# Token-ordered loads of B and C by chunk, and one TensorE stretch per pair of chunks, in a Mamba-2 scan that feeds a GELU MLP

## The chip, the cores and the metric

One core of one Trainium2 chip. The metric is device time in microseconds (us); the profile adds the span of one profiled execution, which is about 2 us shorter than the time of the same run. Ratios are the mean time of one kernel's fast runs over that of the other's fast runs of the same rounds, with a 95% interval, so they are not quite the ratio of the medians that I quote. "Fast" and "slow" are states of a run: here a run over 1.5% above the fastest of its kernel counts as slow. PE is TensorE, DVE VectorE, ACT ScalarE, POOL GpSimd, SP SyncE, whose queue issues nearly all transfers.

## The reference

A gated linear scan in 4 batches of 8 heads, 768 tokens, head size 32, state size 16, then an MLP over all 3072 tokens (256 to 2048 to 256):

```python
for c in range(nc):                         # chunks of the sequence
    cum = np.cumsum(log_a[:, :, sl], axis=-1)
    L = np.exp(cum[:, :, :, None] - cum[:, :, None, :]) * causal
    M = np.einsum('bhin,bhjn->bhij', Cc, Bc) * L                  # Gram, masked
    y_intra = np.einsum('bhij,bhjd->bhid', M, xc)
    y_inter = np.einsum('bhin,bhnd->bhid', Cc, state) * np.exp(cum)[:, :, :, None]
    y[:, :, sl] = y_intra + y_inter
    state = decay_full * state + (B scaled)^T x                   # cut
h = y_tokens @ w_in                         # (3072, 256) @ (256, 2048)
out = gelu_tanh(h) @ w_out                  # (3072, 2048) @ (2048, 256)
```

The kernel works in 24 chunks of 128 tokens. B and C are scaled per token, so the Gram needs only a triangular mask.

## The kernel before

B and C of a whole batch come in one load each, with six neighbouring tokens on one partition. A contiguous run in memory is then 6 x 16 floats, 384 bytes. The price is the order of tokens: the scaled B must be transposed (for the Gram), evicted in token order, and transposed back (for the state product).

```python
def load_bc(b, i, q):                       # one batch, i = 0 for B, 1 for C
    q.dma_start(out=d["bc"][:, i],
                in_=(B, C)[i][b].rearrange("h (p r) n -> p h (r n)", r=R6))
...
def f_N(b, c0, c1):                         # B back to tokens on partitions
    for c in range(c0, c1):
        nc.tensor.transpose(out=bn_ps[...], in_=d["bh"][:, c * Q:(c + 1) * Q], identity=ident)
...
def f_G(gc):                                # Gram of one chunk: four row tiles, 32x128
    for g in range(4):
        nc.tensor.matmul(out=gb[:, g, 0:256], lhsT=d["bh"][32*g:32*g+32, ...],
                         rhs=d["ce"][32*g:32*g+32, :, ...], tile_position=(32 * g, 0))
...
def f_Y(gc):
    for w in range(2):                      # state part: the whole array, 128x128
        nc.tensor.matmul(out=y_ps[:, w], lhsT=sp[:, w*128:(w+1)*128], rhs=d["ch"][...], ...)
    for w in range(2):                      # chunk part: column tiles, 128x32
        for k in range(4):
            nc.tensor.matmul(out=y_ps[32*k:32*k+32, w], lhsT=x16[...], rhs=m[...],
                             tile_position=(0, 32 * k), ...)
    f_D(gc)                                 # state product: column tiles, lhsT = bn
```

Around this lies the MLP: `f_s1` (input product into one of two `hp` buffers in PSUM), `f_gelu` on ACT, `f_s2` (output product into `o_ps`), over groups of one or two chunks. The order of all instructions is fixed at build time by a list scheduler with estimated durations; PE works from that list and waits where the real data is later.

## Time and profile before

| kernel before | |
|---|---|
| time, median of 3 runs | 126.87 us (125.79 to 127.2) |
| span of the profiled execution | 125.3 us |
| PE busy | 117.3 us, 94% |
| first MLP matmul | 15.78 us |

The page cuts the span into 40 slices (3.1 us each), in tenths busy: PE, the granted PE clock, and DMA. Below them are the packets by size.

```profile
PE   5986989899999999999999999999999999999990
...
PEclk9985599999999999999999999999999999999998
...
DMA  3999999819997999931011101010110011001221
...
DMA packets 40047, 13.94 MB, mean 111 GB/s; under 512 B 33824, under 2 KB 39008, under 8 KB 40032
```

PE is at 0.8 or more from the fifth slice on, and the clock is at half in only two slices. DMA is busy for 17 slices, with one hole in the ninth, and then nearly idle. The same in two stretches of the span, with the columns length, then busy time (and count) of PE, weight loads, DVE, ACT, POOL, then granted clock, DMA share and GB/s:

```profile
28.00:40.00 12.00, 11.82 (x146) 9.59 (x145) 8.10 (x12) 7.83 (x16) 2.51 (x6) 1.00 1.02 183
40.00:60.00 20.00, 19.47 (x247) 15.70 (x246) 14.61 (x22) 14.04 (x29) 4.33 (x11) 1.00 0.76 138
```

The two dates to remember, from the timeline (start, length, engine, line, operation): the last cast of the weights `w_out`, and the cast of `x` of chunk 7.

```profile
24.52 0.69 DVE L243 CAST w_out_sb<-wf 128x1024 bf16<-128x1024 f32 x1
```
```profile
32.11 0.40 POOL L241 CAST x_607<-x_t 128x256 bf16<-128x256 f32 x1 [0.52 <-DMA x_t<-in_x_dram]
```

### The profile page before, as it was taken

Reading aid. Unit: us, or ns where it says so; the run is one execution under the profiler, and the core shown is the slowest. Engines: PE = TensorE matmul, PEld = TensorE weight load, DVE = VectorE, ACT = ScalarE, POOL = GpSimd, SP = SyncE. Lnnn points to the kernel's source line nnn. Section 1 sums busy time; section 2 is a strip of 40 time slices with the busy share of each in tenths; the row PEclk is TensorE's granted clock in tenths of the full one; section 3 lists DMA queues with packets and bytes.
Section 4 is the critical chain, followed back from the end, with each engine's and each line's share of the span. In section 5 each row is a group of like instructions: output and inputs, shape, how many; then the busy total and the mean of one; then the engine's idle time right before and its main releaser. Section 6 shows DMA issues by size and latency. Waiting matters only on the chain.

```text
span 125.3 us, 3171 instructions
## 1 busy us (share of the span) xinstructions
PE 117.3 (94%) x1326; PEld 92.3 (74%) x1327; DVE 66.9 (53%) x109; ACT 78.3 (62%) x162; POOL 21.4 (17%) x47
## 2 busy tenths in 40 slices
PE   5986989899999999999999999999999999999990
PEld 2552268689778878768788878787887888988970
DVE  5577777988656799735689650356524500000101
ACT  4021577694668666777749678778678777875110
POOL 6526756102411331111112000000000000000000
PEclk9985599999999999999999999999999999999998
DMA  3999999819997999931011101010110011001221
GB/s 83 264 338 324 297 290 291 196 51 156 164 287 120 170 273 136 153 65 50 7 35 45 42 2 47 0 42 5 42 42 18 29 42 42 25 19 47 84 84 44
DMA packets 40047, 13.94 MB, mean 111 GB/s; under 512 B 33824, under 2 KB 39008, under 8 KB 40032
## 3 DMA queue, kind: packets, MB, share of 16 engines
q1 hardware_dynamic: 38944, 13.29, 45.7%
q10 hardware_dynamic: 1088, 0.44, 1.4%
q8 instruction: 10, 0.16, 0.6%
q14 instruction: 5, 0.04, 0.1%
HBM read 10.58 MB, written 3.15 MB: 110 GB/s over the span
## 4 chain that ended last, share of the span: by engine, by line
PE 85%; DVE 7%; ACT 3%; issue 2%; DVEq 0%
PE hp L439 32%; PE o_ps L457 29%; PE o_ps L694 6%; PE yb L388 4%; PE gb L362 4%; PE hp L457 3%; PE hp L316 2%; DVE m L371 2%; DVE bc_188 L300 2%; PE yb L382 2%; PE yb L348 2%; ACT gT L447 1%; PE gb L268 1%; ACT bn L355 1%; DVE sp_new L420 1%
## 5 line engine op out<-in xcount | busy, mean ns | idle before, releaser
L447 ACT ACTIVATE gT<-hp 128x512 bf16<-128x512 f32 x96 | 55.4, 596 | 18.2 <-PE hp L439 17.4
L439 PE MATMUL hp<-xm,w_in_sb 128*128 128x256 bf16 (+1 forms) x416 | 55.0, 265 | 0.3 <-ACT gT L447 0.2
L457 PE MATMUL o_ps<-w_out_sb,gT 128*128 128x256 bf16 x352 | 50.1, 273 | 0.0
L439 PEld LDWEIGHTS <-w_in_sb 128*128 128x128 bf16 x416 | 36.3, 98 | 6.9 <-issue 0.7
L457 PEld LDWEIGHTS <-gT 128*128 128x128 bf16 x384 | 37.0, 98 | 4.6 <-issue 0.2
L371 DVE TENSOR_TENSOR m<-gb,tri 128x1024 bf16<-128x1024 f32 (+1 forms) x25 | 29.3, 1177 | 12.2 <-PE gb L362 12.0
L466 DVE COPY o_sb<-o_ps 128x256 f32<-128x256 f32 x2 | 0.8, 424 | 22.9 <-PE o_ps L457 22.9
L406 ACT ACTIVATE xm<-yb 128x256 bf16<-128x256 f32 x24 | 9.2, 383 | 5.1 <-PE yb L399 2.1
L420 DVE SCALAR_TENSOR_TENSOR sp_new<-s_new,pend,bmask 128x256 bf16<-128x256 f32 x20 | 10.7, 536 | 0.8
L414 DVE SCALAR_TENSOR_TENSOR s_new<-s_new,pend,yb 128x64 f32<-128x64 f32 x16 | 4.4, 277 | 12.0 <-ACT xm L406 6.1
L694 PE MATMUL o_ps<-wz 128*128 128x512 bf16 x20 | 8.2, 547 | 1.5 <-DVE warm L153 1.3
L464 ACT ACTIVATE o_sb<-o_ps 128x256 f32<-128x256 f32 x20 | 7.6, 381 | 2.8 <-PE o_ps L457 2.5
L362 PE MATMUL gb<-ce,bh 32*128 32x256 bf16 x96 | 7.1, 287 | 0.0
L382 PE MATMUL yb<-ch,sp_new 128*128 128x128 bf16 x40 | 5.5, 219 | 0.3
L355 ACT ACTIVATE bn<-yb 128x384 bf16<-128x384 bf16 (+2 forms) x9 | 4.1, 454 | 2.7 <-PE yb L348 2.7
L241 POOL CAST w_in_sb<-wf 128x1024 bf16<-128x1024 f32 x4 | 4.5, 1132 | 5.6 <-DMA wf<-in_moe_w_in_dram 5.6
L362 PEld LDWEIGHTS <-bh 32*128 32x128 bf16 x96 | 2.4, 91 | 4.0 <-issue 1.7
L694 PEld LDWEIGHTS <-wz 128*128 128x128 bf16 x21 | 2.3, 129 | 3.7 <-issue 2.2
L382 PEld LDWEIGHTS <-sp_new 128*128 128x128 bf16 x40 | 3.8, 98 | 1.0 <-issue 0.6
L457 PE MATMUL hp<-w_out_sb,gT 128*128 128x256 bf16 x32 | 3.8, 272 | 0.0
L464 ACT ACTIVATE o_sb<-hp 128x256 f32<-128x256 f32 x2 | 0.8, 384 | 4.5 <-PE hp L457 4.5
L348 PE MATMUL yb<-ident,bh 128*128 128x128 bf16 x24 | 2.9, 222 | 0.7 <-ACT xm L406 0.3
(157 smaller groups left out, 77.3 us busy)
## 6 DMA issues: line engine op xcount, KB each, us to landing
x_t<-in_x_dram SPq DMA_DIRECT2D x24, 128.0 KB, 3.9
out_dram<-o_sb SPq DMA_DIRECT2D x24, 128.0 KB, 1.7
wf<-in_moe_w_in_dram SPq DMA_DIRECT2D x4, 512.0 KB, 7.9
wf<-in_moe_w_out_dram SPq DMA_DIRECT2D x4, 512.0 KB, 7.2
bc_t<-in_C_dram SPq DMA_DIRECT2D x4, 384.0 KB, 4.3
bc_t<-in_B_dram SPq DMA_DIRECT2D x3, 384.0 KB, 4.9
bc_t<-in_B_dram ACTq DMA_DIRECT2D x1, 384.0 KB, 5.6
a_t<-in_a_dram ACTq DMA_DIRECT2D x1, 48.0 KB, 2.1
```

The lines of the kernel that those rows point to most:

```text
L348: nc.tensor.transpose(out=bn_ps[:, (c - c0) * 128:(c - c0 + 1) * 128], in_=d["bh"][:, c * Q:(c + 1) * Q], identity=ident)
L355: nc.scalar.activation(d["bn"][:, c0:c1].rearrange("p c n -> p (c n)"), bn_ps[:, 0:(c1 - c0) * 128], AF.Copy)
L362: nc.tensor.matmul(out=gb[:, g, 0:256], lhsT=d["bh"][32 * g:32 * g + 32, c * Q:(c + 1) * Q], rhs=d["ce"][32 * g:32 * g + 32, :, c * Q:(c + ...
L371: nc.vector.tensor_tensor(out=state[("m", gc)][:, g0:g1], in0=gram[:, g0:g1], in1=tri_b[:, g0:g1], op=ALU.mult)
L382: nc.tensor.matmul(out=y_ps[:, w], lhsT=sp[:, w * 128:(w + 1) * 128], rhs=d["ch"][:, c * Q:(c + 1) * Q], start=(w == 0), stop=False, skip_ ...
L406: nc.scalar.activation(xm[:, :, gc * Q:(gc + 1) * Q], y_ps, AF.Copy)
L420: nc.vector.scalar_tensor_tensor(out=sp_new.rearrange("p (g d) -> p g d", g=4), in0=state[("s", gc)].rearrange("p (o d) -> p o d", o=1).to ...
L439: nc.tensor.matmul(out=hp[:, j * nt:(j + 1) * nt], lhsT=w_in_sb[:, kc, fi * 128:(fi + 1) * 128], rhs=xm[:, kc, c0 * Q:c0 * Q + nt], start= ...
L447: nc.scalar.activation(gts[g][:, i * per:(i + 1) * per, 0:nt], hps.pop((g, i)).rearrange("p (j t) -> p j t", j=per), AF.Gelu_apprx_tanh)
L457: nc.tensor.matmul(out=ops[gc], lhsT=gts[g][:, fi, tt * Q:(tt + 1) * Q], rhs=w_out_sb[:, fi, :], start=(fi == 0), stop=(fi == NF - 1), ski ...
L464: nc.scalar.activation(o_sb, ops.pop(gc), AF.Copy)
L694: nc.tensor.matmul(out=zb, lhsT=wz[:, 0:128], rhs=wz, start=True, stop=True)
```

## The change

The intent is less work on PE. With B and C in token order, the scaled B is itself the weight of the state product, so the transposes back and their evictions go. Both parts of Y are then column tiles of one shape. From the pair of chunks 4 and 5 on, Y of one pair, the state product and the Gram of the next are issued in one go, so PE changes its tile shape three times a pair instead of six. The first chunk's work also needs only its own 128 tokens instead of a batch of 768.

```diff
-        q.dma_start(out=d["bc"][:, i],
-                    in_=(B, C)[i][b].rearrange("h (p r) n -> p h (r n)", r=R6))
+        for k in range(n):                       # n chunks of the unit, 128 tokens each
+            q.dma_start(out=BCF[u][:, i, k],
+                        in_=(B, C)[i][b, :, (c + k) * Q:(c + k + 1) * Q, :]
+                        .rearrange("h p n -> p h n"))
...
-    def f_N(b, c0, c1):  ...                     # and f_bn, its eviction on ACT
...
     def f_D(u):                                  # state product
-                             lhsT=U[b]["bn"][:, c, 32 * g:32 * g + 32],
+                                 lhsT=BC16[u][:, 0, k, 2 * g:2 * g + 2].rearrange("p h n -> p (h n)"),
...
     def f_Y(u):                                  # state part, now in column tiles too
-                nc.tensor.matmul(out=y_ps[:, w], lhsT=sp[:, w * 128:(w + 1) * 128], ...)
+                        nc.tensor.matmul(out=y4[32 * j:32 * j + 32, k, w],
+                                         lhsT=sp[:, 32 * h:32 * h + 32],
+                                         rhs=CE[u][:, h % 2, k], ...,
+                                         tile_position=(0, 32 * j))
...
+    MERGE = 3
+            def f_YDG(u):
+                f_Y(u)
+                f_D(u + 1)
+                f_G(u + 1)
...
+    load_x_n(0);  load_w_n(0, 1);  load_bc_n(1);  load_w_n(2, 3);  load_x_n(1)   # order on SP
+    load_bc_n(2); load_x_n(2);  load_w_n(0, 1, o=True);  load_bc_n(3)
+    load_w_n(2, 3, o=True);  load_x_n(3)
```

A run in memory is now 16 floats, 64 bytes.

## The prediction

> **What bounds the kernel now.** I read the busy shares first, then the chain of work that ended last, then stretches of the span, then one chunk of the scan in order of time, then the DMA.
>
> ```profile
> PE 117.3 (94%) x1326; PEld 92.3 (74%) x1327; DVE 66.9 (53%) x109; ACT 78.3 (62%) x162; POOL 21.4 (17%) x47
> ```
> ```profile
> PE 85%; DVE 7%; ACT 3%; issue 2%; DVEq 0%
> ```
> PE is the bound, in busy share and in the chain. But 94% is an average over stages, so I cut the span where chunk 7's Gram ends:
>
> ```profile
> 0.00:28.16 28.16, 24.37 (x261) 15.02 (x263) 20.88 (x41) 14.12 (x33) 12.97 (x28) 0.88 0.91 237
> 28.16:39.88 11.72, 11.54 (x144) 9.34 (x141) 7.82 (x12) 7.55 (x16) 2.51 (x6) 1.00 1.02 183
> 39.88:122.09 82.21, 81.42 (x928) 67.97 (x924) 37.81 (x57) 56.61 (x115) 5.88 (x13) 1.00 0.27 60
> ```
> Columns: length, then busy time of PE, weight loads, DVE, ACT, POOL, then granted clock, DMA share, GB/s. Up to 28 us the DMA is full (0.91) and PE is kept up with filler; after 40 us PE is full and DMA idle. So there are two problems. Late, only less PE work helps. Early, only bytes that arrive sooner help.
>
> The two MLP products, from 39.88 us to the end (first the one into the GELU, then the one out of it):
> ```profile
> 39.88:122.10 82.22, 43.05 (x300) 27.74 (x300) 1.00 0.27 60
> ```
> ```profile
> 39.88:122.10 82.22, 43.95 (x320) 31.03 (x320) 1.00 0.27 60
> ```
> Four of these matmuls take 0.4375 us start to start in the timeline, so 0.109 us each: 620 x 0.109 = 67.8 us. The scan's start-to-start time in the same stretch, summed from the timeline, is 12.6 us (Gram 3.62, state part of Y 3.05, rest of Y 2.10, state product 1.75, transposes 1.41 and 0.66). Together 80.4 of 82.2 us: 1.8 us are waits. The whole MLP costs 352 + 384 full matmuls and 64 half ones: 84.0 us that the change does not touch.
>
> One chunk of the scan on PE:
> ```profile
> 39.20 0.28 PE L382 MATMUL yb<-ch,sp_new 128*128 128x128 bf16 x2
> 39.41 0.29 PE L388 MATMUL yb<-m,x_607 128*32 128x128 bf16 x8
> 39.53 0.20 PE L399 MATMUL yb<-x_607,bn 128*32 128x64 bf16 x4
> 39.66 0.29 PE L362 MATMUL gb<-ce,bh 32*128 32x256 bf16 x4
> 39.88 0.61 PE L439 MATMUL hp<-xm,w_in_sb 128*128 128x256 bf16 x4
> ```
> 0.68 us from 39.20 to 39.88. Four column tiles of 128 columns at once stream in about 0.055 us, so Y's eight need 0.11 (0.12 seen), the four state products of 64 columns 0.03 (0.13 seen), the Gram's 256 columns 0.11 (0.22 seen), the two state matmuls 0.11 (0.21 seen). The excess is 0.1 us at each change of tile shape: 128x128 to 128x32, to 32x128, and back.
>
> **What the Trainium skill says.** "TensorEngine Tiling (Array Packing)", Key Properties: changing the tiling mode, not just the tile, drains the engine. The trace agrees: three changes a chunk, 0.1 us each. "DMA: Bandwidth & Descriptors", Why small descriptors are slow: a fixed overhead per packet beside the bytes. The trace agrees: in the packet records the median is 13 ns at 128 B, 22 ns at 384 B, 47 at 1024 and 87 at 2048 B; the line through the first two gives 10.8 ns at 64 B. "TensorE: Matmul & The Clock Gate", Part 1: the clock halves after about 3.4 us of little PE activity and needs as much to return. The trace shows half clock in the slices from 9.4 to 15.7 us, after PE thinned out.
>
> **The change part by part.**
> (1) PE, late. B and C arrive in token order, so the untransposed scaled B is itself the weight of the state product. The 24 transposes back (0.17 us per three) and their nine ACT copies (4.1 us) go. Y of one pair, state product and Gram of the next become one stretch: three shape changes per pair instead of six. Per pair it streams 4 x 0.107 (both parts of Y; the state part now is column tiles too) + 0.05 + 0.21 (Gram), plus 3 x 0.105: 1.0 us, against 2 x 0.68 = 1.36 now. The four transposes forward stay, 0.22. With the 0.11 of transposes back that is 1.22 for 1.69; a chunk that starts a batch has no state part, so on average about 1.2 against 2 x 0.787 (15.3 us of scan over 19.5 chunks from 28 to 115 us) = 1.57. Nine pairs: about 3.4 us off PE.
> (2) DVE and ACT. Per pair DVE does two masks (2 x 1.22), state 2 x 0.28 and 2 x 0.54, scaling about 0.8, two ce copies about 0.54, one bh about 0.28: 5.7 us, an estimate from the present rows. PE takes 7.0 + 1.2 = 8.2 us per pair. ACT: 8 x 0.58 + 0.6 + 0.76 = 6.0. Neither becomes the bound.
> (3) The start. The first scan covers 128 columns of `a`, not 384 (0.95 us now), one transposition matmul replaces 24 (1.47 us now), two scalings of 128 elements replace four of 384 (2.3 us on the chain now), and chunk 0's B and C are 128 KB instead of 768 KB. The first MLP matmul, now at 15.78 us, can come at about 9.5 us. This is hidden work: then it waits for the weights, as the casts of w_in wait for DMA 5.6 us even now.
> (4) DMA, early. Runs of B and C shrink from 384 to 64 B, so 8192 packets become 49152. A chunk's B and C: 2048 packets x 10.8 ns / 16 engines = 1.38 us, for 0.47 (one sixth of 2 x 1.41). In order, with medians plus 4% (before's saturated stretch ran 3% over its medians): `a` ends 2.4 us, B and C of chunk 0 3.8, x 4.7, two w_in quarters 7.6, B and C of chunk 1 9.0, two quarters 11.9, x of chunk 1 12.8, chunks 2 and 3 15.7 and 17.4, two w_out quarters 20.5, B and C of chunks 4 and 5 23.4, w_out 26.5, their x 28.2. w_out's last packets came at 22.2 us before: 4.3 us later now, as six chunks of B and C pass ahead of it at 1.4 us each.
>
> Now the join. Landing is about 1.1 us after the last packet, a cast on POOL 1.04. So the output product of chunk 0 can end at about 29.3 us. By then PE has done the input product of chunks 0 to 3 (7.0 us) and 1.3 us of the output product: 8.3, against 7.9 at 28.2 before. The backlog (rest of the output product of chunks 0 to 3, 5.7 us) lasts to about 34.6. The next input product needs Y of chunks 4 and 5, and that now sits in one stretch with the Gram of chunks 6 and 7, hence waits for their x too. That is 4.6 us of DMA after 28.2: 32.8, or 34.7 if part of it is queued on SP behind the first output store, as loads are now (SP waited 64 us in total at stores). Plus landing 1.1, cast 0.8, hop 0.2: Y starts at 34.9 to 36.8; plus 1.05 of PE, 0.6 of ACT and hops, the input product resumes at 36.7 to 38.6. From there: MLP 84.0 - 14.0 = 70.0, scan nine pairs less what is done 10.3, waits 1.8 as now plus 0.8 to refill the pipe, tail 3.2 (122.1 to 125.3). Sum: 86.1 us. Span 122.8 to 124.7, middle 123.7, against 125.3 profiled.
>
> **The rivals.**
> A: the early DMA is hidden and the PE saving shows in full. For: the saturated queue really ran near its medians, and 64 B packets may cost less than the line says. Then resumption is at 35 us, and the profile is 121, timed 122.5.
> B: the wait moves from engines to DMA and eats the gain. For: 41 thousand more packets, in just the stretch where DMA is already 0.91 full; PE would idle over 3.4 us and return at half clock, 1 to 2 us more. Resumption at 40: profile 126, timed 127.5.
> C: the state product now takes one of the two `hp` buffers that the input product rotates through, until DVE has read it (two ops of 0.28 us and a hop, longer behind a 1.22 us mask). Against: the output product fills such gaps. If it costs 0.2 us in each of eight pairs, 1.6 us, timed 126.5.
>
> **Range and chances.** The profiled execution is 125.3 us, the timed median 126.87, so I add 1.2% to the middle: 123.7 gives 125.2; the chance that A holds is larger than that of B, so I put 124.9 us. The range of 121.9 to 127.2 holds A nearly whole and B's mild form. The line for over 2% faster is 124.3, within half a microsecond of my value: 42% faster, 50% within 2%, 8% slower.
>
> **What would show each step.** (1) start-to-start time from Y of a pair to the next MLP matmul about 1.0 us, and scan PE time late about 1.2 us a pair; wrong if tiles of both parts of Y do not overlap. (3) first MLP matmul at 9 to 10 us. (4) packets of 64 B with a median near 11 ns; the last cast of w_out ending near 28.7 us; x of chunks 6 and 7 cast near 34 to 36 us. The join: a gap on PE of 1 to 3 us before the first stretch of Y, state product and Gram, ended by POOL's cast. C: idle PE before the input product released by DVE's state op. The prediction is wrong if that gap is absent (faster), or if PE waits for DMA again after 42 us (slower).

## The result, and the profile after

| | before | after |
|---|---|---|
| median | 126.91 us (4 runs, 125.79 to 127.2) | 132.49 us (4 runs, 130.7 to 133.25) |
| ratio of fast runs | | 1.035 (1.026 to 1.045), slower |
| span profiled | 125.3 us | 131.3 us |

The change made the kernel slower: the prediction was 124.9 us, with 8% for this side. The profiled run of the kernel after is of the slow state (133.04 us, the fast ones were 130.7 and 131.93), so I checked its dates against two later traces of the same kernel in the fast state: `x` of chunks 6 and 7 is cast at 38.26 us in this one and at 39.13 and 37.85 us in those. The pattern is the same.

First the busy line, and the chain of work that ended last, by engine:

```profile
PE 113.8 (87%) x1404; PEld 89.7 (68%) x1404; DVE 65.5 (50%) x150; ACT 71.4 (54%) x138; POOL 18.5 (14%) x36
```
```profile
PE 70%; SPq 13%; DMA 9%; ACT 1%; DVE 1%; POOL 1%; issue 1%; DVEq 0%
```

PE's busy time fell by 3.5 us (half clock stretches busy time in both kernels, so this is not the work saved), and PE idles for 131.3 - 113.8 = 17.5 us where it idled for 8.0. The sum, 9.5 - 3.5, is the 6.0 us that the span grew. The chain says by whom: before it held no DMA and no SP, now 22% of the span are steps of SP's queue and of transfers. Next the slices and the packets:

```profile
PE   6899663539999955899999999999999999999990
...
PEclk9976999995599999999999999999999999999999
...
DMA  4989969997398799979979978111101111001121
...
DMA packets 81646, 13.94 MB, mean 106 GB/s; under 512 B 75424, under 2 KB 80608, under 8 KB 81632
```

The bytes are the same 13.94 MB, in twice as many packets. DMA is busy for 25 slices instead of 17. PE has holes in slices 5 to 9 and again in 15 to 17 (counted from 1), and it runs at half clock in slices 10 and 11 (28.9 to 35.8 us), after the long holes. The two stretches that answer to those of before:

```profile
28.00:40.00 12.00, 10.38 (x108) 7.26 (x111) 5.03 (x10) 4.32 (x9) 3.31 (x4) 0.72 0.74 115
40.00:60.00 20.00, 16.60 (x246) 13.85 (x235) 12.43 (x30) 10.55 (x21) 1.84 (x3) 1.00 0.90 123
```

Between 28 and 40 us the clock is 0.72 of full, and the DMA share is only 0.74 although many loads are still to come. Between 40 and 60 us PE is 2.9 us less busy than before. What PE waits for (total, times, longest), from the list of waits:

```profile
PE o_ps L475 <- POOL w_out_sb L249: 4.3, 3, 2.2
PE gb L360 <- DVE bh L251: 1.8, 1, 1.8
PE gb L341 <- DVE bh L251: 1.6, 1, 1.6
```

The engines named are only the last link. POOL had itself waited for `w_out` to land, and DVE for B and C. The two dates of before, in the kernel after (in brackets: how long POOL had been idle, and for what):

```profile
29.89 1.04 POOL L249 CAST w_out_sb<-wf 128x1024 bf16<-128x1024 f32 x1 [0.32 <-DMA wf<-in_moe_w_out_dram]
...
38.26 0.61 POOL L249 CAST x<-x_t 128x512 bf16<-128x512 f32 x1 [6.45 <-DMA x_t<-in_x_dram]
```

The last weights are there at 30.9 us instead of 25.2, and x of chunks 6 and 7 at 38.9 instead of 32.5. The second date is a mark of how late the loads are; PE does not stand waiting for that x in any of the three traces of this kernel. The other two waits belong together, at 49 to 53 us. The chain of waits shows the second (start, length, what), and below it stands DVE's own row for the scaling:

```profile
48.60 0.43 SPq L148
...
49.08 2.64 DMA bc_t<-in_C_dram
...
51.81 0.42 DVE bc L321
...
52.76 0.21 DVE bh L251
...
53.01 0.40 PE gb L360 x8
```

```profile
51.81 0.42 DVE L321 TENSOR_TENSOR bc<-bc_t,pt 128x256 bf16<-128x256 f32 x1 [2.40 <-DMA bc_t<-in_C_dram]
```

A load of C is issued at 48.6 us and lands after 2.6 us. Counted through the records, it is C of chunks 12 and 13, while the Gram that waits is that of chunks 8 and 9 and does not use it. The link is the fixed order of work on DVE: DVE stood 2.4 us at the scaling of this C, and behind it stood the eviction of the transposes of chunks 10 and 11 (`ce` and `bh`), which lie in a part of the PSUM tile (`gb`) that the Gram writes. The first wait, 1.6 us, has the same form, with B of chunks 10 and 11. The step ahead of the load in the chain is an output store on SP's queue that waited for a GELU. So a late load stops PE again, well after the weights are in, and it does so for data that PE does not need yet.

What the change was made for did happen. One merged stretch, from the timeline:

```profile
58.94 0.30 PE L403 MATMUL yb<-ce,sp_new 128*32 128x128 bf16 x8
...
59.39 0.20 PE L381 MATMUL hp<-x,bc 128*32 128x64 bf16 x4
59.53 0.40 PE L360 MATMUL gb<-ce,bh 32*128 32x256 bf16 x8
59.86 0.61 PE L458 MATMUL hp<-xm,w_in_sb 128*128 128x256 bf16 x4
```

From Y at 58.94 to the next MLP matmul at 59.86: 0.92 us for a pair (the next stretch takes 0.95). Summed start to start between 60 and 100 us, without the 0.2 us of waits in each, the scan takes 7.5 us of PE before and 5.6 us after.

### The profile page after: what moved, and what is told of

It reads as the page before. It is cut to its first block, busy times and chain, and to the rows that moved or that the text cites. A ratio compares the mean times of both kernels' runs of the same rounds, so it can differ in the third digit from the quotient of the medians.

```text
span 131.3 us, 3378 instructions
## 1 busy us (share of the span) xinstructions
PE 113.8 (87%) x1404; PEld 89.7 (68%) x1404; DVE 65.5 (50%) x150; ACT 71.4 (54%) x138; POOL 18.5 (14%) x36
## 2 busy tenths in 40 slices
DMA packets 81646, 13.94 MB, mean 106 GB/s; under 512 B 75424, under 2 KB 80608, under 8 KB 81632
## 4 chain that ended last, share of the span: by engine, by line
PE 70%; SPq 13%; DMA 9%; ACT 1%; DVE 1%; POOL 1%; issue 1%; DVEq 0%
PE hp L458 30%; PE o_ps L475 29%; DMA wf<-in_moe_w_out_dram 7%; SPq L148 6%; SPq L239 4%; PE gb L360 3%; PE yb L475 3%; DMA bc_t<-in_C_dram 2%; SPq L231 2%; PE yb L403 2%; PE yb L412 2%; SPq L243 2%; PE gb L341 1%; ACT gT L466 1%; POOL w_out_sb L249 1%
## 5 line engine op out<-in xcount | busy, mean ns | idle before, releaser
L249 POOL CAST x<-x_t 128x512 bf16<-128x512 f32 (+1 forms) x12 | 7.1, 596 | 46.6 <-DMA x_t<-in_x_dram 32.3
L421 ACT ACTIVATE xm<-yb 128x512 bf16<-128x512 f32 (+1 forms) x13 | 7.3, 564 | 8.2 <-PE yb L412 5.4
L349 DVE TENSOR_SCALAR ce<-gb,par 128x256 bf16<-128x256 bf16 (+1 forms) x24 | 7.2, 340 | 9.1 <-PE gb L341 9.1
L431 DVE SCALAR_TENSOR_TENSOR s_new<-s_new,pend,hp 128x64 f32<-128x64 f32 x16 | 4.5, 280 | 10.3 <-PE hp L381 10.1
L321 DVE TENSOR_TENSOR bc<-bc_t,pt 128x256 bf16<-128x256 f32 (+1 forms) x13 | 5.2, 399 | 5.0 <-DMA bc_t<-in_C_dram 5.0
L341 PE MATMUL gb<-ident,bc 128*128 128x128 bf16 x46 | 4.9, 220 | 3.2 <-DVE bh L251 1.6
L321 DVE TENSOR_TENSOR bc<-bc_t,rt 128x256 bf16<-128x256 f32 (+1 forms) x12 | 4.9, 409 | 4.8 <-DMA bc_t<-in_B_dram 4.8
L341 PEld LDWEIGHTS <-bc 128*128 128x128 bf16 x48 | 3.6, 98 | 5.0 <-DVE bc L321 2.9
L412 PE MATMUL yb<-m,x 128*32 128x128 bf16 x192 | 6.3, 223 | 0.0
L403 PE MATMUL yb<-ce,sp_new 128*32 128x128 bf16 x160 | 5.3, 221 | 0.0
## 6 DMA issues: line engine op xcount, KB each, us to landing
x_t<-in_x_dram SPq DMA_DIRECT2D x24, 128.0 KB, 3.2
out_dram<-o_sb SPq DMA_DIRECT2D x24, 128.0 KB, 1.7
```

Of the source, the lines that this page charges most:

```text
L249: nc.gpsimd.tensor_copy(out=o, in_=i)
L321: (nc.vector if eng == "DVE" else nc.gpsimd).tensor_tensor(out=BC16[u][:, i, 0:n], in0=BCF[u][:, i, 0:n], in1=w.rearrange("p c (h o) -> p ...
L341: nc.tensor.transpose(out=TT[(u, j)][:, j, k], in_=BC16[u][:, j, k].rearrange("p h n -> p (h n)"), identity=ident)
L403: nc.tensor.matmul(out=y4[32 * j:32 * j + 32, k, w], lhsT=sp[:, 32 * h:32 * h + 32], rhs=CE[u][:, h % 2, k], start=first(j), stop=False, t ...
L412: nc.tensor.matmul(out=y4[32 * j:32 * j + 32, k, w], lhsT=X16[u][:, k, 32 * h:32 * h + 32], rhs=m[:, h // 2, h % 2, :], start=first(j), st ...
```

## The experiments

There were 14 runs, in four calls, each beside the kernel before on the same chip. Where a kernel gives wrong values on purpose I say so; its shapes, its work and its waits are those of the kernel it came from. My theory after reading the traces: the 64-byte packets make the early transfers so late that PE stalls and its clock halves. The rivals: the merge itself (Y of a pair now waits for x, B and C of the next pair), the clock alone, and the order of issue on SP. Comparisons with the control are made between fast runs, so they can differ from those of the medians quoted.

### The kernel after, again

No edit; it is the control of the first call.

> The changed kernel once more, as the base for the others on this chip: 1.03 to 1.045 of the kernel before. The profile should again show w_out's third quarter cast near 28.5 us, half clock near 29 to 36 us and the first merged stretch near 39.5 us.

Measured: 135.18 us (134.62 to 135.89) against 125.59; ratio 1.076 (1.069 to 1.084). That is above the first ratio, 1.035. The trace (fast state) shows why the ratio moves. The clock is at half in two places this time, 23.8 to 34.0 us and 51.1 to 57.9 us:

```profile
PEclk9999999555999996589999999999999999999998
```

So the size of the loss varies from chip to chip, and the places of the clock drops with it. Kernels of one call are compared below; where I compare across calls I say so.

### The same bytes in long runs

```diff
-                        in_=(B, C)[i][b, :, (c + k) * Q:(c + k + 1) * Q, :]
-                        .rearrange("h p n -> p h n"))
+                        in_=flat[(c + k) * Q * H * N:(c + k + 1) * Q * H * N]
+                        .rearrange("(p f) -> p f", p=128))       # 512 B a partition; wrong values
```

> The changed kernel with the same bytes of B and C in runs of 512 B (128 packets a load instead of 1024); its values are wrong on purpose. Theory D (small packets of B and C fill the DMA and the SP queue, so weights and x land late): w_out's last cast ends 4 to 6 us earlier, the first merged stretch comes near 33 us, and the time falls by 5 to 8 us, to 0.97 to 1.00 of the kernel before. Theory K (the half clock and PE's fixed order cost it) and theory M (the merged stretch waits for the next pair): at most 1.5 us faster than the changed kernel.

Measured: 124.03 us (122.5 to 125.91), ratio to before 0.977 (0.970 to 0.984); against the control of the same call the fast runs (two of its four) take 122.65 us for 135.22, a ratio of 0.907, or 12.6 us less; I had expected 5 to 8. Profile:

```profile
PEclk9999999599999999999999999999999999999998
...
DMA  2999899825685687576782210111011101111021
```
```profile
31.40 0.61 POOL L250 CAST x<-x_t 128x512 bf16<-128x512 f32 x1 [6.55 <-DMA x_t<-in_x_dram]
```

With nothing changed but the length of the runs, x of chunks 6 and 7 is there 7.7 us earlier than in the control (31.40 for 39.13), the DMA is no longer full, and half clock shrinks to 21.1 to 24.5 us. The short runs account for the whole loss: with long runs this kernel is below before.

### No merge

```diff
-    MERGE = 3
+    MERGE = NU                                  # never; Y, state product and Gram apart
-    st = ctx.enter_context(tc.tile_pool(name="st", bufs=4))
+    st = ctx.enter_context(tc.tile_pool(name="st", bufs=12))
```

> The changed kernel with Gram and state products of each pair on their own again, and 12 instead of 4 buffers for the states, which that needs. Theory M: Y of chunks 4 and 5 comes 3 to 5 us earlier than 39.5 us and the time falls by 2 to 4 us. Theory D: the input product still waits for w_out and x, so at most 1 us is gained early, and about 0.2 us a pair is lost late by one more change of tile shape: within 1 us of the changed kernel.

Measured: 138.98 us (137.69 to 140.32), ratio 1.104; between fast runs 138.55 us for 135.22, 1.025 of the control. Neither theory had expected a loss of 3.3 us. The first Y of chunks 4 and 5 now does come 5 us earlier (34.31 us for 39.37), as the merge theory says, and yet the kernel is slower. PE waits elsewhere:

```profile
PE hp L381 <- POOL x L249: 3.9, 6, 1.0
```

The state product alone waits six times for x. The merge is not what costs. (The schedule orders PE and SP anew in this run, so it is no clean price of the merge.)

### Fillers to hold the clock

Seventeen idle matmuls ahead of the first quarters of chunk 0's output product, where PE waits for `w_out`.

```diff
+        if u == 0 and q < 3:
+            for _ in range((4, 3, 10)[q]):
+                nc.tensor.matmul(out=yb, lhsT=wz[:, 0:128], rhs=wz, start=True, stop=True)
```

> The changed kernel with 17 filler matmuls of 512 columns in the three waits of chunk 0's output product for w_out, into the yb bank, free then. Theory K (half clock from 29 to 36 us costs 3 us): full clock there and the time falls by 2.5 to 3.5 us. Theory D: the clock stays full, but the first merged stretch still starts when x of chunks 6 and 7 is cast, near 39 us, so the gain is under 1 us.

Measured: 132.45 us (131.7 to 134.57), ratio 1.053, so between fast runs 132.20 us for 135.22, 3.0 us less than the control. In its trace (a run of the slow state) the clock holds from 19.2 to 49.9 us; it is at half from 15.8 to 19.2 us and from 49.9 to 56.8 us. The x of chunks 6 and 7 is still cast at 38.00 us. The gain is what the theory of the clock alone had expected (2.5 to 3.5 us), the late x what the other had. So the clock is a real part, but the smaller one beside the 12.6 us of the long runs; the drops come after waits.

### Long runs early, long runs late

The edit of the long runs for chunks 0 to 5 only (`u < 4`), or only for the later ones (`u >= 4`); both give wrong values.

> Runs of 512 B for B and C of chunks 0 to 5 only, 64 B for the rest (values wrong on purpose). If the loss is made before w_out has landed, this has nearly all the gain of the run with 512 B everywhere: 0.98 to 1.00 of the kernel before. If the loads of the later chunks cost as much, about half: near 1.02 to 1.03.

> The converse: 64 B for chunks 0 to 5, 512 B for the rest (values wrong on purpose). If the loss is early: 1.05 to 1.07 of the kernel before, so 1 to 3 us faster than the changed kernel, the waits for scaled B and C near 46 to 53 us gone. If it is late: near 1.02.

Before was noisy in this call (124.83 to 128.0), and the kernel after was not run in it. Long runs early: 127.96 us (125.22 to 130.78) for before's 127.12; its only fast run took 125.22 us, level with before's three (125.51 on average), and gave no ratio. Its last `w_out` cast starts at 23.22 us and x of chunks 6 and 7 is cast at 33.77 us. Long runs late: 130.79 us (128.95 to 132.16), ratio 1.031 (1.005 to 1.058), with those dates at 30.75 and 39.36 us, as in the kernel after. So long runs early gain more than long runs late. Early ones alone do not give the 0.977 that long runs everywhere had on another chip, so the late packets seem to count too. The intervals are too wide, and the chips too different, for a split in numbers.

### B issued from ACT

```diff
-            bl[(u, i)] = load(..., load_bc, u, i, nc.sync, deps=deps)
+            bl[(u, i)] = load(..., load_bc, u, i, nc.scalar if i == 0 and u < 4 else nc.sync, deps=deps)
```

> The changed kernel, right values, with the B loads of chunks 1 to 5 issued from ACT instead of SP. If the DMA engines' packets are the limit, it stays within 1% of the changed kernel (1.04 to 1.08). If SP's issue in order, which showed waits of 2 to 4 us per issue while DMA was below 0.8 busy, is the limit, w_out's last cast ends 2 us earlier or more and the time falls by 2 to 4 us.

Measured: 136.16 us, ratio 1.084 (1.071 to 1.097). The last cast of `w_out` does start 3 to 4 us earlier (26.67 us), but x of chunks 6 and 7 comes no earlier (40.00 us), and PE waits 4.4 us for ACT's `xm`, since ACT is held up by its own issues. A second issuing engine moves the delay around; it does not remove it.

### The converse: short packets in the kernel before

```diff
-        q.dma_start(out=d["bc"][:, i], in_=(B, C)[i][b].rearrange("h (p r) n -> p h (r n)", r=R6))
+        for r in range(R6):
+            q.dma_start(out=d["bc"][:, i, :, r * N:(r + 1) * N], in_=src[:, :, r])   # 64 B runs; correct
```

> The kernel before, right values, with each of its eight loads of B and C cut into six of 1024 packets of 64 B, as many packets as the changed kernel has. Theory D: it loses as the changed kernel does, 8 to 14 us, 1.06 to 1.11; the first MLP matmul comes 5 us later since all of batch 0 is loaded first. If the 64 B packets are not the cause: within 2 us.

Measured: 138.12 us (137.81 to 139.95), ratio 1.101 (1.075 to 1.127).

```profile
DMA packets 81647, 13.94 MB, mean 102 GB/s; under 512 B 75424, under 2 KB 80608, under 8 KB 81632
```

The number of packets is that of the kernel after, within one, in a kernel that has nothing else of the change, and between fast runs it loses 12.5 us (138.02 for 125.51). B and C also come in 48 loads here instead of 8, as in the kernel after; the run with long runs keeps those 48 and loses nothing, so their number is not the cause. Together the two runs show the cause from both sides.

### Long runs and no merge

The two edits above together; wrong values.

> 512 B runs for B and C (values wrong on purpose) and the products of a pair not merged, so that the merge is seen without the late loads. If the merge saves its changes of tile shape: 2 to 4 us slower than the run with 512 B alone, near 1.00 of the kernel before. If the merge is worth nothing or costs by its waits: the same as that run, 0.97 to 0.98, or faster.

Measured: 128.89 us (128.45 to 129.19), ratio 1.024 (1.018 to 1.030). The kernel with long runs and the merge had 0.977, on another chip: 1.024 / 0.977 = 1.048. That would be about 6 us for the merge, more than my 3.4 us off PE. But between chips the kernel after alone moved from 1.035 to 1.076 of before, so this size is not shown. Nor is the merge the only difference: without it the schedule changes too, the first output store is issued at 30.75 us for 27.35, and x of chunks 6 and 7 is cast at 35.11 us for 31.40. Between 60 and 100 us the scan takes 6.5 us of PE without the merge and 6.0 with it. The rest I did not take apart.

### The stores on ACT's queue

```diff
-        nc.sync.dma_start(out=out[gc * Q:(gc + 1) * Q, :], in_=o_sb)
+        (nc.scalar if eng == "ACT" else nc.sync).dma_start(out=out[gc * Q:(gc + 1) * Q, :], in_=o_sb)
```

> The changed kernel, right values, with the output stores issued from ACT instead of SP, so that no load waits behind a store for its data. If the 2 us hole in the loads near 34 us, when SP waits for the first output, is a large part of the loss: x of chunks 6 and 7 is cast 2 to 3 us earlier and the time falls by 2 to 4 us. If the packets alone decide: within 1.5 us of the changed kernel.

Measured: 143.43 us, ratio 1.139 (1.132 to 1.145), the slowest of all. x of chunks 6 and 7 is cast at 37.31 us, 0.5 to 2 us earlier than in the three traces of the kernel after, but the GELU engine now stands:

```profile
ACT gT L466 <- DMA bc_t<-in_C_dram: 7.0, 2, 5.0
```

ACT's GELU waits up to 5.0 us. ACT's own store stands before it, issued at 38.09 us, 4.6 us after its data was there; what held it is not shown, though the wait ends with a load. PE waits 9.7 us for the GELU. This run could not tell whether SP's order costs anything, so I made another.

### All loads ahead of the first store, and no pacing

A control, the kernel after with every load issued on SP before the first store (and 16 output buffers for 6), and the kernel after without the pacing of the later loads.

```diff
     def f_oev(gc, eng):
+        for once in pending.values():           # every load not yet issued
+            once()
```
```diff
-            load_bc_n(u, deps=[Gn[u - 4]])
+            load_bc_n(u)
```

> The kernel after, unchanged, as the control of this call, because its ratio to the kernel before was 1.035 on one chip and 1.076 on another. Expected 1.03 to 1.08, with x of chunks 6 and 7 cast at 38 to 40 us and one more wait for B and C of later chunks between 46 and 54 us.

> The kernel after with every load issued on SyncE ahead of the first output store, and 16 output buffers in place of 6, so that no load stands behind a store that waits for its data. If the late loads come from the order on SyncE, x of chunks 6 and 7 is cast at about 36.5 us (37.3 when the stores went to ScalarE's queue), the waits for B and C after 42 us are gone, and the time falls by 2 us or more against the control of this call. If the packets themselves are the limit, x of 6 and 7 comes within 1.5 us of the control, the DMA stays full to about 70 us, and the time is within 2% of the control. A third possibility is that stores held behind some 35 us of loads stall the engines by buffers: then it is slower.

> The kernel after without the pacing of the later loads: each pair's B and C no longer wait in the schedule for the Gram of four units earlier, and the stores keep their place by time. SyncE theory: the waits for B and C after 42 us go, 1 to 3 us faster than the control. Packet theory: the first stretch of Y stays at 38 to 40 us, as the packets ahead of it are the same; only the later wait can go, at most 1.6 us.

Measured: control 133.37 us (ratio 1.063), loads first 130.44 us (1.039), no pacing 134.04 us (1.057; between fast runs 132.65 for 133.33, no effect). Loads first gains 130.44 / 133.37 = 0.978. x of chunks 6 and 7 is cast at 37.37 us for the control's 37.85, and PE still waits for B and C at 47.6 and 50.5 us (1.6 and 1.1 us, in the control 2.3 and 0.9). So at the first merged stretch the order on SP is worth half a microsecond only. The other difference is the clock: both have one drop between 24 and 33 us, the control has two more (15 to 22 us and 49 to 57 us), this kernel none. So part of its 2.9 us is clock drops that did not happen. How much I cannot separate.

The same trace shows what remains. Two of its windows, in which SP issues one load after another with no store between them:

```profile
32.00:34.00 2.00, 2.00 (x22) 1.60 (x20) 2.00 (x3) 1.91 (x4) 0.29 (x1) 1.00 0.56 52
...
42.00:44.00 2.00, 2.00 (x22) 1.79 (x20) 0.93 (x3) 1.72 (x4) 0.30 (x1) 1.00 0.46 42
```

The DMA share is only 0.56 and 0.46 there, and nearly all of it is 64-byte packets. So loads of 64-byte packets leave the 16 engines idle part of the time without any store in the way. Whether the issue on SP or the engines set that pace is not settled. In the kernel after, SP's last issue before the store ended at 32.44 us, and the 1334 packets still to come, 0.88 us of packet time on 16 engines, took until 33.98 us; there, at least, SP's issuing was over.

### A version that beats both

The kernel before with its 384-byte loads and its chunks 0 to 3, and from chunk 4 on the merged stretch; the transposes of a whole batch go to the Gram's banks. Correct values.

```diff
+    P0 = 4                                      # first chunk of the merged pairs
+                lhsT=U[b]["bn"][:, c, 32 * g:32 * g + 32]       # the transposes back stay
+                    def f_YDG(c0):
+                        f_Y2(c0)
+                        f_D2(c0 + 2)
+                        f_G2(c0 + 2)
```

> A kernel of both, right values: loads of B and C in 384 B runs and everything up to chunk 3 as in the kernel before; from chunk 4 on Y of a pair, state product and Gram of the next pair are one stretch as in the changed kernel, fed by the transposes of a whole batch. If the merged stretch saves PE time as reckoned (0.25 us a chunk pair after the 0.1 for the transposes back, ten pairs) and only the packets cost: 0.975 to 0.99 of the kernel before. If the merged stretch itself brings waits that eat this: 0.995 to 1.02.

Measured: 123.91 us (6 runs, 122.23 to 124.83) against 127.22, between fast runs 122.65 against 125.79; ratio 0.976 (0.965 to 0.988). The verdict at the 2% line is "unclear", but the interval lies below 1.

```profile
PE 112.4 (93%) x1429; PEld 90.4 (75%) x1429; DVE 65.3 (54%) x109; ACT 75.5 (63%) x149; POOL 21.7 (18%) x47
```
```profile
PEclk9999999999999999999999999999999999999999
```

PE's busy time is below that of the kernel after, although the transposes back are still there, and the clock never drops in this execution. The gain of the change did not need its loads. This kernel also has more buffers and makes the transposes of a whole batch at once in the Gram's banks; what these are worth was not taken apart from the merged stretch.

## Why the prediction was wrong

Its closing sum against the trace of the kernel after. The MLP still to do is 656 matmuls x 0.109 us; "scan" is the start-to-start sum without waits; the waits are what is left. This trace is of the slow state, with half clock up to 35.8 us, before the point where the sum starts:

| term | predicted, us | in the trace, us |
|---|---|---|
| input product resumes after the first merged stretch | 37.6 (36.7 to 38.6) | 41.35 |
| MLP still to do | 70.0 | 71.8 |
| scan on PE | 10.3 | 9.3 |
| waits | 2.6 | 5.1 |
| tail | 3.2 | 3.75 |
| span | 123.7 | 131.3 |

**(1) PE, late: right.** 0.92 to 0.95 us a stretch for the 1.0 predicted, and the scan term is 1 us better than reckoned. The runs without the merge were slower by more than this, but they are no clean measure of it.

**(2) DVE and ACT: right.** Neither became the bound; both stay under 55% busy.

**(3) The start: too early, without consequence.** The first MLP matmul came at 12.04 us, not 9.5, and before at 15.78. As predicted it was hidden work: PE then waited for weights, 0.8 us for `w_in` and 4.3 us for `w_out`.

**(4) DMA, early: the first failed step.** The cost of a packet was right (median 11 ns, mean 10.8, for 10.8), and so was their number (81646 - 40047 = 41599 more, for 40960). The error was to add them up as if the engines were never idle between loads, plus 4%. From the packet records, w_in's last packet came at 13.5 us for 11.9, w_out's at 29.5 for 26.5. Four loads of 1024 such packets, from 30.4 to 34.0 us, took 3.6 us, 0.90 us each, where their packets fill only 0.69 us of 16 engines. The windows of the kernel after show the rest:

```profile
30.00:32.00 2.00, 2.00 (x16) 0.93 (x15) 0.77 (x1) 0.00 (x0) 1.54 (x2) 0.50 0.75 80
32.00:34.00 2.00, 2.00 (x11) 1.44 (x10) 1.59 (x2) 1.30 (x3) 0.00 (x0) 0.50 0.74 69
34.00:36.00 2.00, 2.00 (x15) 1.18 (x14) 1.03 (x4) 0.87 (x2) 0.00 (x0) 0.56 0.22 71
```

The share is 0.75 on 64-byte loads, then 0.22 while SP stands at the first output store. I had kept that store as a maybe of 1.9 us; the control and the kernel with loads first put it at 0.5 us.
**The join: the second failed step.** I had expected PE to finish its backlog at 34.6 us and then to wait 1 to 3 us for the cast of x of chunks 6 and 7. That gap is absent:

```profile
38.55 1.04 PE L475 MATMUL o_ps<-w_out_sb,gT 128*128 128x256 bf16 x8
39.52 0.29 PE L403 MATMUL yb<-ce,sp_new 128*32 128x128 bf16 x8
```

PE works without a break from 29.62 us to Y at 39.52, and in both fast traces Y starts before the cast of that x has ended (39.37 and 38.06 us, for casts that end at 39.74 and 38.46), since Y stands first in the stretch and does not use it. PE was late by itself. Its list puts the output product of chunk 0, which needs `w_out`, ahead of most of the input product of chunks 2 and 3. So it stood at `w_out` for 4.3 us in three waits, the last of them up to 29.62 us, although both `hp` buffers had been read by 28.07 us. By then it had done 48 full matmuls of the MLP, 5.25 us of work for the 8.3 us of the prediction, and the backlog that remained began at half clock. So "Y starts at 34.9 to 36.8" became 39.52. The prediction's own sign, an absent gap, was to mean a faster kernel; it did not. A list built with the measured times of the transfers was not tried.

**The clock: under-sized.** The sentence "PE would idle over 3.4 us and return at half clock, 1 to 2 us more" stood in rival B, and B is what held, with a low chance and a mild price (resumption at 40 us and a profile of 126, for 41.35 and 131.3). In the three windows above the clock is 0.50, 0.50 and 0.56: PE is busy the whole time. The 6.8 us at half clock are worth 3.4 us of work at full clock, by my estimate. The waits and this are why 71.8 us of MLP were left instead of 70.0, and fillers alone won back 3.0 us in the first call.

**After the join: the prediction's own test of its error came true.** It said that it is wrong "if PE waits for DMA again after 42 us". It does, for late loads by way of DVE's order, 1.6 and 1.8 us at 49.5 and 53.0 us; these 3.4 us are more than the 2.5 us by which the waits exceed the sum. My own figures, 4.6 us of DMA beside 8.2 us of PE for a pair, had made the later transfers look hidden; they started so late that twice they were not.

Rival A is refuted: early DMA was not hidden. Rival C, the `hp` buffer, is not seen in the kernel after: its list of waits has no wait of the input product for DVE. The run with fillers has one of 0.2 us, and 2.5 us of it appear only when the merge is taken out.

## What to carry to other kernels

A change of layout that spares the busiest engine work must be priced at the transfer too: count packets, not bytes, and where the DMA is already full early, leave room for short packets to cost more than their own time, as they did here. When a change joins two ideas, try each alone; here the kernel with the merged stretch and the old loads gains 2.4%, and the short packets alone lose 10%. In these traces a late transfer cost twice on TensorE, once as the wait and again as half clock after it. And when each engine works from a fixed list, ask what stands behind a late transfer on that list: here PE and DVE both stood at data that the work behind it did not need.

## What the Trainium skill lacked or had wrong

- "DMA: Bandwidth & Descriptors", Why small descriptors are slow, gives a fixed overhead per packet; that agrees here (11 ns median at 64 B for 22 ns at 384 B). That section gives no rate for whole loads of 64-byte packets: here 0.90 us per load of 1024 packets, for 0.69 us of packet time, and DMA shares of 0.46 to 0.75 in stretches of them with more loads to come.
- "DMA: Bandwidth & Descriptors", Issuing engines are not separate DMA queues, says that issuing from several engines only saves time on the sequencer. It lacks what the second issuer can lose, whatever the reason: with the stores issued from ACT, a GELU waited 5.0 us and the kernel took 1.139 of before.
- "TensorE: Matmul & The Clock Gate", Part 1, puts the ramp penalty at less than 1% of a typical kernel's span. That is said of the warm-up, and the same part tells of drops in waits for DMA, so this is a caution and no error: here half clock lasted 6.8 to 10.2 us at a time, twice in one execution of 133.9 us and once in another after the first 12 us, and fillers ahead of three of the waits won 3.0 us, 2%.
